# A transformer block on one core: the feed-forward's block 12 of the last tokens in row tiles of 64, and their last product, addition and store in two halves of columns

## The chip, the core and the metric

The kernel runs on one core of one Trainium2 chip. The metric is the device time in microseconds of one launch, input and output in device memory. A core has TensorE (PE; its weight loads are listed as PEld), VectorE (DVE), ScalarE (ACT), GpSimd (POOL) and SyncE (SP, which here issues all transfers); each works through a queue of its own, in order, and waits for the others through semaphores. TensorE writes its results into PSUM, eight banks of 2 KB in each of the 128 partitions.

## The reference

A transformer block on 2048 tokens of width 448: attention with 16 heads of 28 that share one key and one value head, then a gated feed-forward of width 1792, each behind a layer norm and with a residual. Cut to what matters:

```
def _A_ref(x, wq, wk, wv, wo):
    q = (x @ wq).reshape(B, S, H, Dh).transpose(0, 2, 1, 3)
    k, v = x @ wk, x @ wv
    p = softmax(einsum("bhqd,bkd->bhqk", q, k) * Dh ** -0.5)
    o = einsum("bhqk,bkd->bhqd", p, v)
    return o.transpose(0, 2, 1, 3).reshape(B, S, H * Dh) @ wo

def _B_ref(x, w1, w3, w2):
    h = silu(x @ w1) * (x @ w3)
    return h @ w2

h = x + _A_ref(_layernorm(x), wq, wk, wv, wo)
h2 = h + _B_ref(_layernorm(h), w1, w3, w2)
```

All is float32. To keep that accuracy the kernel splits an operand into a high part (rounded to the type `F32R`) and the rest, and adds up three products: high x high, low x high, high x low (`PAIRS3`).

## The kernel before

**Tiles.** The tokens are in NT = 4 tiles of T = 512 (index t), each of NQ = 4 groups of 128 tokens (index n). The width D = 448 is three chunks of 128 and one of 64. The feed-forward's 1792 hidden columns are NF = 14 blocks of 128 (index k). The attention comes first; the feed-forward follows as one loop over t and k, and the change touches its last two blocks, k = 12 and 13 of the last tile (`tl` = 3), and what stands behind the loop.

**One block.** For (t, k) there is a first product (x by w1 and by w3, into two PSUM banks of 512 columns), then `hidden` (L1030), then a second product with w2 that adds into the four banks Y[t][0..3], one for each group of 128 tokens, 448 columns used of 512. `hidden` is a chain over two engines: silu on ACT (L1032), multiplication on DVE (L1034), a copy that rounds to the high part on ACT (L1039), the subtraction for the low part on DVE (L1040). Its result goes into a buffer of `pt_ring` (L820), a ring of four of which each block takes two: first one for silu's result, then one for the high and low parts. Block k + 2 gets the buffers of block k again. A write to such a buffer waits for every earlier reader, also for one that is issued later in the program's text but belongs to the buffer's previous use.

**Two forms of a block.** The full form: `ffn1` (L1043) makes 2 x 11 matmuls of 128 rows through `mm_D` (L159; matmul L166), `ffn2` (L1065; matmul L1070) makes three matmuls for each n. The form in row tiles of 64: `ffn1_half` and `ffn2_half` (L1054, L1073) cut the 128 rows into two halves of 64 and issue pairs of matmuls, one on each half of the array, through `two` (matmul L1024); the two matmuls of a pair run side by side and write to different banks. Each is called twice, first with `late` = 0 and then with 1, and in the second call the two halves of rows have changed banks. `ffn1_half` has 11 pairs in the early and 10 in the late call, `ffn2_half` 6 in each. Since two halves of the array must not write one bank at the same time, each such call but the late one of `ffn1_half` ends with `settle` (L1027): ACT reads one element of the bank that was written last, and the next matmul into that bank waits for this read.

**The order around the change.** The order of every engine's queue is the order of the program's text. In a half block (t, k) it is: `ffn1_half` early, `ffn2_half` early of the block before, `ffn1_half` late, `hidden` of this block, then `rest()`, which is `ffn2_half` late of the block before; then `split_w2` (L488), which prepares this block's w2. So the second product lags one block behind. With the last tile the loop before takes blocks 0 to 11 in half form. Blocks 12 and 13 (`end`) are full: `ffn1(12)`, `ffn1(13)`, and the second products of 11, 12 and 13 stand behind the loop, all full. After each group n of the last product, `y_out` (L1087) adds the residual on DVE (L1092) and issues the store of X[tl][:, n] on SP (L1095).

```
    def settle(ps):
        se.activation(pexp[:1, 8:9], ps[:1, :1], AF.Copy)

        y, eng = Y[t][n][:, :D], ve
        eng.tensor_tensor(X[t][:, n], y, X[t][:, n], op=ALU.add)
        sy.dma_start(ov[t][:, n], X[t][:, n])
```

Of the kernel before, what the change touches and what calls it, by code (L numbers as in the profile page):

```python
# [11 lines left out]
ALU = mybir.AluOpType  # L12
# [4 lines left out]
P = 128  # L17
S = 2048
D = 448
# [5 lines left out]
NQ = T // P  # L25
NG = H // 4
NC = S // P
NF = F // P
# [7 lines left out]
def block_kernel(  # L36
# [13 lines left out]
    ve, se, ge, pe, sy = nc.vector, nc.scalar, nc.gpsimd, nc.tensor, nc.sync  # L50
    xv = x[0].rearrange("(t p n) d -> t p n d", t=NT, p=P, n=NQ)
    ov = out[0].rearrange("(t p n) d -> t p n d", t=NT, p=P, n=NQ)
# [14 lines left out]
    X = [keep.tile([P, NQ, D], F32, name=f"X{t}") for t in range(NT)]  # L67
# [75 lines left out]
    def bank(name="pb"):  # L143
        k = min(free, key=lambda k: order[k])
        free.remove(k)
        if k < 7:
            ps = ps_w.tile([P, T], F32, name=name, tag=f"bank{k}")
        else:
            ps = ps_o.tile([P, T], F32, name="po")
        used[id(ps)] = ps, k  # L150
        ready.pop(id(ps), None)
        return ps

    def done(ps, at=None):
        k = used.pop(id(ps))[1]
        order[k] = ready.get(id(ps), clock.end) + 0.7 if at is None else at
        free.append(k)
# [137 lines left out]
    QS, MX, MR, PT, PO, WH, WS = {}, {}, {}, {}, {}, {}, {}  # L295
# [183 lines left out]
    def split_w(k):  # L479
        wh, wl = [qs_tile().rearrange("p a (c m e) -> p (a c) m e", c=2, m=2)  # L480
                  for b in range(2)]
        ve.tensor_copy(wh, W13[k])
        ge.tensor_tensor(wl, W13[k], f(wh), op=ALU.subtract)
        return wh, wl
# [3 lines left out]
    def split_w2(k, own=False):  # L488
        if own or not w2s_home and k == 0:
            w2s = qs_tile()[:, :, 16 : 16 + D]  # L490
        else:
            if not w2s_home:
                w2s_home.append(keep.tile([P, 2, 2, T], F32R, name="w2s", tag="ks1"))
            w2s = w2s_home[0][:, k % 2, :, 16 : 16 + D]
        ve.tensor_copy(w2s[:, 0], W2[k])
        ge.tensor_tensor(w2s[:, 1], W2[k], f(w2s[:, 0]), op=ALU.subtract)
        return w2s
# [380 lines left out]
    for s in range(AHEAD, LAST):  # L878
        i, c = divmod(s, NC)
        n, kt = divmod(c, NQ)  # L880
# [128 lines left out]
    HID, Y = {}, {}  # L1009
# [5 lines left out]
    PAIRS3 = ((0, 0), (1, 0), (0, 1))  # L1015
    FULL = 4
# [13 lines left out]
    def hidden(t, k, ps, then=None):  # L1030
        sg = f(pt_ring()[:, 0])
        se.activation(sg, ps[0], AF.Silu)  # L1032
        done(ps[0])
        ve.tensor_tensor(sg, ps[1], sg, op=ALU.mult)  # L1034
        done(ps[1])
        if then is not None:
            then()
        h = pt_ring()
        se.activation(h[:, 0], sg, AF.Copy)  # L1039
        ve.tensor_tensor(h[:, 1], sg, f(h[:, 0]), op=ALU.subtract)  # L1040
        HID[t, k] = h[:, 0], h[:, 1]

    def ffn1(t, k, W):  # L1043
        ps = [bank("pa"), bank("pa")]
        for m in range(2):
            mm_D(ps[m], ps[m], [w[:, :, 1 - m] for w in W], XT[t], slice(0, P), slice(0, T))
        hidden(t, k, ps)
# [6 lines left out]
    def ffn1_half(t, k, W, ps, late):  # L1054
        us = [products(t, W, late, 0), products(t, W, 1 - late, 1)]
        if not late:
            us[0].append((W[1][HALF[0], 3, 1], XD[t][HALF[0]]))
            us[1].append((W[1][HALF[1], 3, 0], XT[t][2][HALF[1], 3]))
        to = (ps[0], ps[1]) if not late else (ps[1], ps[0])
        two([[(to[h], *u, not late and x == 0, late and x == len(us[h]) - 1) for x, u in enumerate(us[h])]  # L1060
             for h in range(2)])
        if not late:
            settle(ps[1])

    def ffn2(t, k, n):  # L1065
        if n == 0 and k == 0:
            Y[t] = [bank() for _ in range(NQ)]
        hid, w2s = HID[t, k], WS[t, k]
        for m, (a, b) in enumerate(PAIRS3):
            pe.matmul(Y[t][n][:, :D], hid[a][:, n * P : (n + 1) * P], w2s[:, b],  # L1070
                      start=(k == 0 and m == 0), stop=(k == NF - 1 and m == 2), skip_group_check=True)

    def ffn2_half(t, k, late):  # L1073
        if k == 0 and not late:
            Y[t] = [bank() for _ in range(NQ)]
        hid, w2s = HID[t, k], WS[t, k]
        us = [[], []]
        for h in range(2):
            for n0 in (2, 0) if late else (0, 2):
                n, r = n0 + (h ^ late), HALF[h]  # L1080
                for m, (a, b) in enumerate(PAIRS3):
                    us[h].append((Y[t][n], hid[a][r, n * P : (n + 1) * P], w2s[r, b],
                                  not late and k == 0 and m == 0, late and k == NF - 1 and m == 2))
        two(us)
        settle(Y[t][0 if late else 3])

    def y_out(t, n):  # L1087
        y, eng = Y[t][n][:, :D], ve
        if t < NT - 1 and n > 1:
            y, eng = ln_pool.tile([P, 512], F32, name="xn", bufs=4)[:, :D], ge  # L1090
            se.activation(y, Y[t][n][:, :D], AF.Copy)
        eng.tensor_tensor(X[t][:, n], y, X[t][:, n], op=ALU.add)  # L1092
        done(Y[t][n])
        if t == NT - 1:
            sy.dma_start(ov[t][:, n], X[t][:, n])  # L1095
        elif n == NQ - 1:
            sy.dma_start(ov[t], X[t])

    tl = NT - 1
# [5 lines left out]
    def call(*at):  # L1105
        for fn, args in after.get(at, []):
            fn(*args)
# [24 lines left out]
    prev = None  # L1132
    for t in range(NT):
        for k in range(NF):
            end = t == tl and k >= NF - 2
            t2, k2 = divmod(NF * t + k + 2, NF)
            if t2 < NT:
                WH[t2, k2] = split_w(k2)
            W = WH.pop((t, k))
            if t == 0 and k < FULL or end:  # L1140
                ffn1(t, k, W)
                call(t, k)
                if prev is not None and not end:
                    for n in range(NQ):
                        ffn2(*prev, n)
            else:
                ps = [bank("pa"), bank("pa")]
                ffn1_half(t, k, W, ps, 0)
                ffn2_half(*prev, 0)
                ffn1_half(t, k, W, ps, 1)  # L1150

                def rest():
                    ffn2_half(*prev, 1)
                    if prev[1] == NF - 1:
                        for n in range(NQ):
                            y_out(prev[0], n)

                hidden(t, k, ps, rest if prev[1] == NF - 1 else None)
                call(t, k)
                if prev[1] != NF - 1:  # L1160
                    rest()
            t2, k2 = divmod(NF * t + k + 1, NF)
            if t2 < NT:
                WS[t2, k2] = split_w2(k2, end)
            call(t, k + 0.5)
            prev = (t, k)
    for n in range(NQ):
        ffn2(tl, NF - 3, n)
    for n in range(NQ):
        ffn2(tl, NF - 2, n)  # L1170
    for n in range(NQ):
        ffn2(tl, NF - 1, n)
        y_out(tl, n)


# [26 lines left out]
```

## Time and profile before

| | |
|---|---|
| median of three runs | 1160.41 us (1159.94 to 1161.62) |
| the profiled execution | 1160.38 us |
| its span, first to last instruction | 1158.6 us |
| granted TensorE clock, mean | 1.000 |
| stores of the last tile | 4 issues, 224 KB each |

The span lies within the profiled execution's own time; 1.8 us are outside it. In the profile's rows a line such as `PE L1024 MATMUL pb<-w2s,pt 64*128 64x448 f32 x7` names the engine, the line of the kernel, the operation, the tile written and the tiles read, rows by columns of the array used, the shape of the moving operand and the count; ahead of it stand the start in the span and the time from the first one's start to the last one's end, both in microseconds. In brackets behind it stands the idle time of the engine ahead of it and what ended that. A matmul's record covers its way through the array, so neighbours overlap; their pace is the distance of their starts. A number in brackets behind a windows column counts instructions. The PSUM tiles `pa`, `pb` and `po` are banks under the names that they were first given: Y[tl][0] is listed as `po` and Y[tl][1..3] as `pb` at the end, `pt` is a buffer of the ring, `pexp` the place that `settle` writes to.

### The profile page before, as it was taken

How to read it: one execution, taken by the hardware profiler on the slowest of the kernel's cores; microseconds unless marked ns; L12 is line 12 of the kernel's file. 1: busy time of each engine (PE TensorE's matmuls, PEld its weight loads, DVE VectorE, ACT ScalarE, POOL GpSimd, SP SyncE). 2: the span in 40 equal slices, each digit the busy share in tenths (PEclk: the TensorE clock that was granted, in tenths of full speed). 3: DMA queues.
4: the chain of work that ended last, by engine and by line, in shares of the span. 5: the costliest groups of instructions: out<-in, count | busy, mean ns of one | idle time of the engine just before them, and what ended most of it. 6: DMA issues, size and time to landing. Idle time of an engine off the chain costs nothing.

```text
span 1158.6 us, 25640 instructions
## 1 busy us (share of the span) xinstructions
PE 1149.0 (99%) x10154; PEld 772.7 (67%) x10154; DVE 805.8 (70%) x1498; ACT 764.3 (66%) x1587; POOL 330.2 (29%) x242
## 2 busy tenths in 40 slices
PE   8999999999999999999999999999999999999998
PEld 6664444446444445444445444589999999999997
DVE  8878999897999998999988983163543444344333
ACT  5649999997999997999997999512222222222221
POOL 5312001101101111110111011345565556556552
PEclk9999999999999999999999999999999999999999
DMA  4010100001000002000012100143211101000000
GB/s 168 10 38 1 34 13 18 19 15 47 19 12 10 19 24 54 19 20 3 19 24 55 50 19 14 56 103 96 73 39 20 41 1 49 17 33 33 1 1 33
DMA packets 66680, 38.15 MB, mean 33 GB/s; under 512 B 41728, under 2 KB 59392, under 8 KB 66560
## 3 DMA queue, kind: packets, MB, share of 16 engines
q1 hardware_dynamic: 66560, 36.51, 11.5%
q8 instruction: 79, 1.29, 0.5%
q14 instruction: 41, 0.34, 0.1%
HBM read 24.04 MB, written 7.47 MB: 27 GB/s over the span
## 4 chain that ended last, share of the span: by engine, by line
PE 94%; ACT 2%; DVE 2%; issue 1%; DMA 1%; SPq 0%; POOL 0%; ACTq 0%; POOLq 0%
PE po L423 21%; PE pb L407 20%; PE pa L1024 18%; PE pa L323 10%; PE pb L1024 9%; PE pa L166 5%; PE pb L166 4%; PE po L1024 4%; PE pb L1070 1%; ACT OT L430 1%; ACT ab L344 1%; DVE mx L333 1%; PE pb L273 0%; ACT pt L414 0%; PE po L166 0%
## 5 line engine op out<-in xcount | busy, mean ns | idle before, releaser
L333 DVE TENSOR_REDUCE mx<-pa 128x1 f32<-128x512 f32 x689 | 440.1, 685 | 22.1 <-PE pb L407 13.0
L407 PE MATMUL pb<-qs,KS 32*128 32x512 f32 x3072 | 384.9, 425 | 0.0
L414 ACT ACTIVATE pt<-pb 128x512 f32<-128x512 f32 x684 | 365.9, 621 | 20.1 <-PE pb L407 17.3
L407 PEld LDWEIGHTS pb<-qs,KS 32*128 32x128 f32 x3072 | 234.0, 182 | 132.2 <-ACT pt L414 66.9
L323 PE MATMUL pa<-KS,qs 32*128 32x512 f32 x886 | 311.7, 459 | 1.3
L1024 PE MATMUL pa<-xl,qs 64*128 64x512 f32 x1044 | 195.4, 388 | 0.0
L323 PEld LDWEIGHTS pa<-KS,qs 32*128 32x128 f32 x886 | 138.6, 182 | 83.6 <-DVE mx L333 46.3
L423 PE MATMUL po<-pt,VA 128*32 128x512 f32 x1368 | 182.2, 605 | 0.4 <-ACT pt L414 0.4
L1024 PE MATMUL pa<-xh,qs 64*128 64x512 f32 x739 | 159.9, 388 | 0.0
L454 POOL TENSOR_TENSOR OT<-OT,rb 128x512 f32<-128x512 f32 x15 | 19.7, 1311 | 458.1 <-DMA rb<-sd 240.9
L1024 PE MATMUL pb<-w2s,pt 64*128 64x448 f32 x1050 | 145.2, 360 | 0.0
L1034 DVE TENSOR_TENSOR pt<-pa,pt 128x512 f32<-128x512 f32 x49 | 33.8, 691 | 159.0 <-ACT pt L1032 152.9
L1024 PEld LDWEIGHTS pa<-xl,qs 64*128 64x128 f32 x1044 | 141.9, 184 | 3.1
L1024 PEld LDWEIGHTS pb<-w2s,pt 64*128 64x128 f32 x1050 | 125.2, 184 | 2.0 <-DVE pt L1040 0.2
L351 DVE CUSTOM_DVE_ANT_0 ab<-pa,ab 128x512 f32<-128x512 f32 x138 | 93.6, 686 | 39.5 <-PE pa L323 28.4
L1024 PEld LDWEIGHTS pa<-xh,qs 64*128 64x128 f32 x739 | 108.4, 184 | 3.2
L414 ACT ACTIVATE xl<-pb 128x512 f32<-128x512 f32 x170 | 99.6, 610 | 8.9 <-PE pb L407 6.8
L414 ACT ACTIVATE xh<-pb 128x512 f32<-128x512 f32 x170 | 104.5, 633 | 0.0
L1032 ACT ACTIVATE pt<-pa 128x512 f32<-128x512 f32 x49 | 29.3, 597 | 94.7 <-PE pa L1024 90.9
L423 PE MATMUL po<-xl,VA 128*32 128x512 f32 x340 | 89.4, 605 | 0.0
L423 PE MATMUL po<-xh,VA 128*32 128x512 f32 x340 | 89.4, 605 | 0.0
L344 ACT ACTIVATE ab<-pa 128x512 f32<-128x512 f32 x138 | 82.2, 608 | 6.7 <-PE pa L323 4.9
(156 smaller groups left out, 1411.4 us busy)
## 6 DMA issues: line engine op xcount, KB each, us to landing
rb<-sd SPq DMA_DIRECT2D x64, 64.0 KB
xr<-xn SPq DMA_DIRECT2D x64, 56.0 KB
QR<-OT SPq DMA_DIRECT2D x60, 56.0 KB
QR<-in_B_w_dram SPq DMA_DIRECT2D x16, 192.0 KB
xh<-xr SPq DMA_DIRECT2D x4, 768.0 KB
X<-in_A_x_dram SPq DMA_DIRECT2D x3, 896.0 KB
out_dram<-X SPq DMA_DIRECT2D x3, 896.0 KB
w<-in_B_w_dram SPq DMA_DIRECT2D x8, 192.0 KB
```

Source lines behind the costliest of these rows:

```text
L166: pe.matmul(ps, lhs[b][:, cb, lsl], (rhs[2] if ca == 3 and len(rhs) == 3 else rhs[a])[:, ca, rsl], start=(k == 0), stop=(k == len(terms) - 1),
L323: pe.matmul(ps, QS[i][r, 0, n * P : (n + 1) * P], KS[0][r, kt * T : (kt + 1) * T] if keys is None else keys[r], start=True, stop=True)
L333: ve.tensor_reduce(self.to(), ps, axis=AX.X, op=ALU.max)
L344: se.activation(self.ab, ps, AF.Relu)
L351: ve.tensor_tensor_reduce(self.ab, ps, self.ab, 1.0, -3.0e38, ALU.add, ALU.max, self.to())
L407: pe.matmul(self.ps, KS[k % 2][r, c * P : (c + 1) * P], QS[i][r, k // 2], start=(k == 0), stop=(k == 2))
L414: se.activation(f(PT[i, c, p][:, jj]), self.ps, AF.Exp, bias=0.0, scale=SCALE)
L423: pe.matmul(PO[i][32 * j : 32 * j + 32], VA[:, c], f(PT[i, c, j // 2][:, j % 2]), start=(c == 0), stop=(c == NC - 1))
L454: eng.tensor_tensor(o, o, rb, op=ALU.mult)
L1024: pe.matmul(ps[:, : rhs.shape[-1]], lhs, rhs, start=bool(first), stop=bool(last), skip_group_check=True)
L1032: se.activation(sg, ps[0], AF.Silu)
L1034: ve.tensor_tensor(sg, ps[1], sg, op=ALU.mult)
```

## The change

Block 12 of the last tile takes the half form: only block 13 is still full. Block 12's iteration does not call `rest()`, so the late half of block 11's second product moves behind the loop, behind `ffn1(13)` and `hidden` of 13, and is followed by the full second products of 12 and 13. Of the last product's group n = 3, the three matmuls, the addition and the store are each done twice, for columns 0 to 223 and 224 to 447, in the order matmuls, addition, store, matmuls, addition, store; both halves lie in the one bank of Y[tl][3].

```
@@ -1137,7 +1137,7 @@
             if t2 < NT:
                 WH[t2, k2] = split_w(k2)
             W = WH.pop((t, k))
-            if t == 0 and k < FULL or end:
+            if t == 0 and k < FULL or (t, k) == (tl, NF - 1):
                 ffn1(t, k, W)
                 call(t, k)
                 if prev is not None and not end:
@@ -1157,20 +1157,27 @@
 
                 hidden(t, k, ps, rest if prev[1] == NF - 1 else None)
                 call(t, k)
-                if prev[1] != NF - 1:
+                if prev[1] != NF - 1 and (t, k) != (tl, NF - 2):
                     rest()
             t2, k2 = divmod(NF * t + k + 1, NF)
             if t2 < NT:
                 WS[t2, k2] = split_w2(k2, end)
             call(t, k + 0.5)
             prev = (t, k)
-    for n in range(NQ):
-        ffn2(tl, NF - 3, n)
+    ffn2_half(tl, NF - 3, 1)
     for n in range(NQ):
         ffn2(tl, NF - 2, n)
-    for n in range(NQ):
+    for n in range(NQ - 1):
         ffn2(tl, NF - 1, n)
         y_out(tl, n)
+    hid, w2s = HID[tl, NF - 1], WS[tl, NF - 1]
+    for h in range(2):
+        sl = slice(h * D // 2, (h + 1) * D // 2)
+        y = Y[tl][NQ - 1][:, sl]
+        for m, (a, b) in enumerate(PAIRS3):
+            pe.matmul(y, hid[a][:, (NQ - 1) * P :], w2s[:, b, sl], start=False, stop=(m == 2), skip_group_check=True)
+        ve.tensor_tensor(X[tl][:, NQ - 1, sl], y, X[tl][:, NQ - 1, sl], op=ALU.add)
+        sy.dma_start(ov[tl][:, NQ - 1, sl], X[tl][:, NQ - 1, sl])
```

More of the change, by code (lines that the diff above doesn't have):

```diff
@@ L1139, in block_kernel @@
             W = WH.pop((t, k))
-            if t == 0 and k < FULL or end:
+            if t == 0 and k < FULL or (t, k) == (tl, NF - 1):
                 ffn1(t, k, W)
@@ L1159, in block_kernel @@
                 call(t, k)
-                if prev[1] != NF - 1:
+                if prev[1] != NF - 1 and (t, k) != (tl, NF - 2):
                     rest()
@@ L1166, in block_kernel @@
             prev = (t, k)
-    for n in range(NQ):
-        ffn2(tl, NF - 3, n)
+    ffn2_half(tl, NF - 3, 1)
     for n in range(NQ):
         ffn2(tl, NF - 2, n)
-    for n in range(NQ):
+    for n in range(NQ - 1):
         ffn2(tl, NF - 1, n)
         y_out(tl, n)
+    hid, w2s = HID[tl, NF - 1], WS[tl, NF - 1]
+    for h in range(2):
+        sl = slice(h * D // 2, (h + 1) * D // 2)
+        y = Y[tl][NQ - 1][:, sl]
+        for m, (a, b) in enumerate(PAIRS3):
+            pe.matmul(y, hid[a][:, (NQ - 1) * P :], w2s[:, b, sl], start=False, stop=(m == 2), skip_group_check=True)
+        ve.tensor_tensor(X[tl][:, NQ - 1, sl], y, X[tl][:, NQ - 1, sl], op=ALU.add)
+        sy.dma_start(ov[tl][:, NQ - 1, sl], X[tl][:, NQ - 1, sl])
 _INS = ["A_x", "A_wq", "A_wk", "A_wv", "A_wo", "B_w1", "B_w3", "B_w2"]
```

## The prediction

> **What bounds the kernel now.** I read the page first: its span, the busy row and the chain that ended last.
>
> ```profile
> span 1158.6 us, 25640 instructions
> PE 1149.0 (99%) x10154; PEld 772.7 (67%) x10154; DVE 805.8 (70%) x1498; ACT 764.3 (66%) x1587; POOL 330.2 (29%) x242
> PE 94%; ACT 2%; DVE 2%; issue 1%; DMA 1%; SPq 0%; POOL 0%; ACTq 0%; POOLq 0%
> ```
>
> TensorE is busy 99% of the span and carries 94% of the chain: a matmul taken off its queue, or a gap put into it, shows one to one. The change touches only the end, so next comes the chain of the last 21 us (start, length, what).
>
> ```profile
> 1137.51 10.19 PE pa L166 x44
> 1147.70 0.61 PE po L1070 x3
> 1148.31 1.80 PE pb L1070 x9
> ...
> 1152.51 0.61 PE po L1070 x3
> ...
> 1153.15 2.43 DVE X L1092 x4
> ```
>
> Blocks 12 and 13 (44 matmuls of 512 columns), then the second products of blocks 11, 12 and 13, 12 matmuls of 448 columns each: block 11's take 0.61 + 1.80 us, so 0.200 us a matmul. After 1153.15 the four additions set the end. Behind them stand the stores; the windows view gives the share of the DMA engines (last two columns: share, GB/s).
>
> ```profile
> core 0: us, PE busy (x) PEld busy (x) DVE busy (x) ACT busy (x) POOL busy (x), PEclk, DMA share, GB/s
> 1154.50:1155.00 0.50, 0.41 (x3) 0.04 (x1) 0.50 (x2) 0.00 (x0) 0.00 (x0) 1.00 0.67 251
> 1155.00:1155.50 0.50, 0.00 (x0) 0.00 (x0) 0.50 (x1) 0.00 (x0) 0.00 (x0) 1.00 1.03 380
> ...
> 1157.00:1157.50 0.50, 0.00 (x0) 0.00 (x0) 0.00 (x0) 0.00 (x0) 0.00 (x0) 1.00 0.23 83
> 1157.50:1158.60 1.10, 0.00 (x0) 0.00 (x0) 0.00 (x0) 0.00 (x0) 0.00 (x0) 1.00 0.00 0
> ```
>
> The engines move data from 1155.00 - 0.67 x 0.5 = 1154.67 to 1157.00 + 0.23 x 0.5 = 1157.12, without a pause. Four stores of 224 KB in 2.45 us are 374 GB/s, 0.61 us each; 1.48 us more pass to the end of the span.
>
> **Part 1: block 12 in row tiles of 64.** A half block's period is the distance of two silu starts; the pace of full matmuls comes from rows of blocks 12 and 13.
>
> ```profile
> 1129.11 0.60 ACT L1032 ACTIVATE pt<-pa 128x512 f32<-128x512 f32 x1 [1.79 <-PE pa L1024]
> ...
> 1136.33 0.60 ACT L1032 ACTIVATE pt<-pa 128x512 f32<-128x512 f32 x1 [2.07 <-PE pa L1024]
> ...
> 1136.94 0.57 PE L1024 MATMUL po<-w2s,pt 64*128 64x448 f32 x2
> ...
> 1137.43 0.53 PEld L166 LDWEIGHTS pa<-xl,qs 128*128 128x128 f32 x3 [0.31 <-issue]
> ...
> 1138.23 0.85 PE L166 MATMUL pa<-xh,qs 128*128 128x512 f32 x3
> ...
> 1146.40 0.84 PE L166 MATMUL pa<-xl,qs 128*128 128x512 f32 x3
> ...
> 1147.09 0.62 PE L166 MATMUL pa<-xh,qs 128*128 128x512 f32 x2
> ```
>
> Of the 44 matmuls 3 start before 1138.23 and 5 from 1146.40 on: 8.17 us / 36 = 0.227 us. Removed: 22 x 0.227 + 12 x 0.200 = 7.39 us. Added: one period, 7.22 us, with both of its halves of the second product. **Gain 0.17 us**: the 64 rows left over of 448 = 3 x 128 + 64 take 21 slots of pairs where full tiles take 22. Its own waits (the two settles, HID of the block before) stand where every half block has them, within the period.
>
> **Mode switches.** Before there is one, half to full. The second of the two matmuls at 1136.94 starts at 1137.14, so the next slot would be 1137.34; counted back from 1138.23 (3 x 0.227) it is 1137.55: 0.21 us. The other direction occurs once, behind the last wo_rows:
>
> ```profile
> 773.30 2.39 PE L166 MATMUL pa<-WO,OS 128*128 128x448 f32 x11
> ...
> 775.62 0.18 PEld L1024 LDWEIGHTS po<-xl,qs 64*128 64x128 f32 x1 [0.31 <-issue]
> ...
> 775.96 0.39 PE L1024 MATMUL po<-xl,qs 64*128 64x512 f32 x1
> ```
>
> The eleventh ends at 775.69, so starts at 775.33 (a matmul of 448 columns is 0.57 - 0.20, say 0.36 us long); its successor's slot would be 775.53, and is 775.96 - 0.23 = 775.73: 0.20 us. After the change the order is: half block 12, full ffn1 of 13, late half of block 11's product, full products of 12 and 13. Three switches for one: **+0.20 us** here, and one more that falls into the wait that follows.
>
> **The new wait.** ffn2_half ends with settle(Y[0]), a 1x1 read by ACT; the next matmul, ffn2(12, 0), writes Y[0] and has to wait for it. In ACT's queue settle stands behind the cast of block 13 (L1039), which is emitted earlier, in hidden(13). That cast writes the pt buffer that holds block 11's hidden (a ring of 4, two per block), so it can't start until the last matmul of block 11's product has read it:
>
> ```profile
> 1148.75 1.36 PE L1070 MATMUL pb<-w2s,pt 128*128 128x448 f32 x6
> ...
> 1150.15 0.63 ACT L1039 ACTIVATE pt<-pt 128x512 fp32r<-128x512 f32 x1 [4.24 <-PE pb L1070]
> ```
>
> Before, this costs nothing: block 12's product runs on meanwhile. After, TensorE itself waits for cast and settle. Their prices:
>
> ```profile
> 1137.69 0.63 ACT L1039 ACTIVATE pt<-pt 128x512 fp32r<-128x512 f32 x1 [0.76 <-DVE pt L1034]
> ...
> 1138.22 0.14 ACT L1028 ACTIVATE pexp<-po 1x1 f32<-1x1 f32 x1
> ```
> ```profile
> 857.04 0.81 DVE L1040 TENSOR_TENSOR pt<-pt 128x512 fp32r<-128x512 f32 x1 [0.21 <-ACT pt L1039]
> ...
> 857.90 0.18 PEld L1024 LDWEIGHTS po<-w2s,pt 64*128 64x128 f32 x1 [0.20 <-DVE pt L1040]
> 857.90 0.47 PE L1024 MATMUL po<-w2s,pt 64*128 64x448 f32 x1
> ```
>
> From the start S of the last half matmul: its end +0.36, cast starts +0.04 (1150.11 to 1150.15), settle starts +0.53 (1137.69 to 1138.22) and takes 0.14, the weight load follows +0.05 (857.85 to 857.90), and a matmul whose load was not ahead loses 0.11 (0.47 against 0.36, the length of a matmul of 448 columns). The next slot is S + 1.23 in place of S + 0.20: **+1.03 us**, the switch within it. Bounds: +0.20 if nothing waits, and 1.03; the rows name each link, so I take 1.03. Behind the waiting matmul stand all 24 of blocks 12 and 13. The other input of that cast, the multiplication (L1034), starts 0.10 us after ffn1's end and takes 0.69; block 11's late half ends 1.4 us after it (switch and 6 slots of 0.200), so the cast waits for TensorE, not for DVE. DVE's subtraction behind the cast has 2.4 us of block 12's product as cover. The skipped rest() frees 1.20 us of TensorE between block 12 and 13; silu and multiplication of 12 then lie beside ffn1 of 13 (5.0 us), which needs neither.
>
> Sum on TensorE: -0.17 + 0.20 + 1.03 = **+1.06 us** at the start of the last products.
>
> **Part 2: the last product in two halves of columns.** The rows:
>
> ```profile
> 21.75 1.75 PE L273 MATMUL pb<-ident,xn 128*128 128x128 f32 x14 [0.18 <-DVE xn L213]
> ```
> ```profile
> L1034 DVE TENSOR_TENSOR pt<-pa,pt 128x512 f32<-128x512 f32 x6 | 4.1, 691 | 23.0 <-ACT pt L1032 16.9 <-PE pa L166 6.1
> ...
> L1092 DVE TENSOR_TENSOR X<-pb,X 128x448 f32<-128x448 f32 x3 | 1.8, 626 | 0.0
> ```
> ```profile
> 1153.75 1.83 DVE L1092 TENSOR_TENSOR X<-pb,X 128x448 f32<-128x448 f32 x3
> 1153.80 2.14 SPq L1095 DMA_DIRECT2D out_dram<-X  x4
> ```
>
> The trace has no matmul of 224 columns. Transposes, with a full weight load and 128 columns each, go at most 1.75 / 14 = 0.125 us apart, and 0.200 less 224 x 0.42 ns (0.227 - 0.200 over 64 columns) is 0.11: I take 0.11 each, at most 0.20. An addition of 224 columns: 65 ns per 64 columns, so 626 - 228 = 0.40 us. By the clock of before: the three additions in the row start 0.60 us apart, so the third of the four ends at 1154.98, and addition A, though its matmuls end near 1154.65, runs from 1154.96 to 1155.36.
>
> Does the second half's product wait for A? It is emitted behind A and writes other columns of the same PSUM tile, one bank (2 KB a partition). The trace shows no such pair; the nearest rows are matmuls into a bank whose reader is not done:
>
> ```profile
> PEld pb L407 <- ACT pt L414: 66.9, 87, 0.8
> ```
>
> So between 0 and the full price I take the wait. Then: load 1155.41, slot 1155.52, third matmul 1155.74 to 1156.01 (0.36 less 224 x 0.42 ns), addition B 1156.03 to 1156.43. The first store is issued at 1153.80 and moves data from 1154.67, 0.87 us later; B's moves from 1157.32, 0.31 us, to 1157.63, where before it ends at 1157.12: **+0.52 us**. Store A (data from 1156.48) is done by then. Without the wait B's addition ends at 1155.74, its data at 1157.09, since the engines are full up to there: 0.0. Outer bounds: slots of 0.20 us for both halves would add 0.3; half-length packets may go slower, by the 512-byte loads (140 GB/s at a share of 0.48, so 292) 0.39 us in place of 0.31:
>
> ```profile
> 776.00:778.00 2.00, 2.00 (x20) 1.68 (x18) 0.95 (x2) 0.00 (x0) 0.97 (x1) 1.00 0.48 140
> ```
>
> SP has one issue more; four span 2.14 us at the pace of the additions that they wait for, and A's and B's come 0.4 us or more apart, so I cost it at nothing; without that cover it is one issue, at most 2.14 - 3 x 0.60 = 0.34 us.
>
> The Trainium skill, page "PSUM — Partial Sum Buffer", section "PSUM bank collisions raise a hardware error", speaks against this split: two engines may not touch one bank in the same 32 partitions at once, even in disjoint columns, so software has to guard by bank. By that rule the halves can't overlap and the total is the forecast; without it, it would be the first rival's. No run here shows it yet.
>
> **Sum.** 1.06 + 0.52 = +1.58 us. The profiled execution took 1160.38 us (span 1158.6), the median of the three is 1160.41: so **1162.0 us**, 0.14% more. About 0.2% (2.3 us) is what a measurement of this kernel can tell from no change; this stays within it.
>
> **Rivals.**
> 1. The halves overlap: +1.06 + 0.0, **1161.4 us**. For it: the columns are disjoint. Against it: one tile, one bank.
> 2. settle doesn't hold TensorE (it, or the cast, runs earlier): -0.17 + 0.20 + 0.20 + 0.52 = +0.75, **1161.1 us**. Against it: the 4.24 us row above.
> 3. Neither wait: +0.23, **1160.6 us**; the change then just does nothing that counts, since the slot saved is spent on switches and the split meets full DMA engines.
> 4. Slower beyond 0.2%: the gaps of 0.8 us and 0.6 us let the granted clock fall for the last products (about 4.9 us of slots). At half clock +4.9: +6.5 in all, **1166.9 us**. It decides from 0.75 us more, a clock below 4.9 / 5.65 = 0.87. Against it: around an idle microsecond at the start (6 to 7) the clock column reads 1.00.
>
> ```profile
> 6.00:7.00 1.00, 0.00 (x0) 0.00 (x0) 0.93 (x4) 0.60 (x1) 0.83 (x3) 1.00 1.08 395
> 7.00:8.00 1.00, 0.79 (x7) 0.79 (x8) 0.93 (x5) 0.16 (x1) 0.56 (x2) 1.00 0.92 133
> ```
>
> **Numbers.** Forecast 0.62, rivals 0.15, 0.08, 0.05 and 0.04, anything else 0.06. The range runs from just below rival 3 to the forecast with both outer bounds of part 2 (+0.4) and half of the 1.7 us by which the three runs differ: 1160.3 to 1163.2. Slower by over 0.2% (above 1162.7): rival 4, an eighth of the forecast through that spread, half of the rest: 0.15. Faster: 0.02, no mechanism found that saves 2.3 us. Within 0.2%: 0.83.
>
> **What would show it.** Right: ACT's cast of block 13 released by an L1024 matmul, settle behind it, then TensorE idle some 0.8 us before the first L1070; its first L1070 1.06 us after the place that block 12's product had; a gap before the last three matmuls released by DVE; an end of data 0.5 us further behind the first L1092. Wrong: the first L1070 follows the last L1024 within 0.4 us; six short matmuls in a row; a block 12 period other than 7.22 less the 1.20 of the late half; a clock below 1.00.

## The result and the profile after

| | before | after |
|---|---|---|
| median of 22 runs each | 1160.28 us | 1161.92 us |
| lowest to highest | 1159.71 to 1161.62 | 1161.43 to 1164.52 |
| ratio, with its 95% interval | | 1.0013 (1.0007 to 1.0019) |
| the profiled execution, its span | 1160.38, 1158.6 | 1162.54, 1160.8 |

The change costs 1.64 us by the medians, 0.14% (by the ratio 0.13%): less than the 0.2% that the prediction gives as what a measurement can tell from no change, yet the interval of the ratio leaves out 1. The forecast was 1162.0 us.

The two spans differ by 2.2 us, more than the change costs. The reason stands ahead of the change: block 11's multiplication (L1034) starts at 1136.96 us in the trace of before and here at

```profile
1137.52 0.69 DVE L1034 TENSOR_TENSOR pt<-pa,pt 128x512 f32<-128x512 f32 x1 [4.24 <-ACT pt L1032]
```

though up to there both programs issue the same. Such a shift differs from one execution to the next (1136.23 to 1137.98 us over the traces of this study), so the end is read in two distances: **a**, from this start to the first matmul of block 13's second product, and **d**, from there to the end of the stores' data. In the timeline of before:

```profile
1136.96 0.69 DVE L1034 TENSOR_TENSOR pt<-pa,pt 128x512 f32<-128x512 f32 x1 [4.24 <-ACT pt L1032]
...
1152.35 0.76 PE L1070 MATMUL po<-qs,pt 128*128 128x448 f32 x3
```

So before, a = 1152.35 - 1136.96 = 15.39 us and d = 1157.12 - 1152.35 = 4.77 us.

The timeline of after where the late half of block 11's product ends (start, length, what, in brackets the idle time and its end):

```profile
1150.36 0.36 PE L1024 MATMUL pb<-w2s,pt 64*128 64x448 f32 x1
1150.37 0.36 PE L1024 MATMUL po<-w2s,pt 64*128 64x448 f32 x1
...
1150.77 0.63 ACT L1039 ACTIVATE pt<-pt 128x512 fp32r<-128x512 f32 x1 [3.31 <-PE po L1024]
1151.30 0.14 ACT L1028 ACTIVATE pexp<-po 1x1 f32<-1x1 f32 x1
...
1151.49 0.50 PEld L1070 LDWEIGHTS po<-w2s,pt 128*128 128x128 f32 x3 [1.14 <-ACT pexp L1028]
1151.50 0.87 PE L1070 MATMUL po<-w2s,pt 128*128 128x448 f32 x3 [0.77 <-ACT pexp L1028]
...
1154.01 0.76 PE L1070 MATMUL po<-qs,pt 128*128 128x448 f32 x3
```

The reader sees the predicted chain link by link: the last half matmul, the cast released by it, settle 0.53 us behind the cast's start, and TensorE idle until settle is done. a = 1154.01 - 1137.52 = 16.49, 1.10 us more than before.

The chain of work that ended last shows the same by engine (start, length, what): ACT, which had no place in this stretch of it before, now bridges the gap (ACTq is ACT's sequencer).

```profile
1150.77 0.63 ACT pt L1039
1151.39 0.06 ACTq L1204
1151.45 0.04 issue
1151.50 0.87 PE po L1070 x3
```

The last product in the timeline, then the stores in the windows view:

```profile
1155.42 1.21 DVE L1092 TENSOR_TENSOR X<-pb,X 128x448 f32<-128x448 f32 x2
...
1155.81 0.49 PE L1178 MATMUL pb<-qs,pt 128*128 128x224 f32 x3
1156.55 0.38 DVE L1179 TENSOR_TENSOR X<-pb,X 128x224 f32<-128x224 f32 x1
1156.98 0.41 PEld L1178 LDWEIGHTS pb<-qs,pt 128*128 128x128 f32 x3 [0.87 <-DVE X L1179]
1156.98 0.59 PE L1178 MATMUL pb<-qs,pt 128*128 128x224 f32 x3 [0.69 <-DVE X L1179]
1157.04 1.33 SPq L1180 DMA_DIRECT2D out_dram<-X  x2
1157.61 0.39 DVE L1179 TENSOR_TENSOR X<-pb,X 128x224 f32<-128x224 f32 x1 [0.69 <-PE pb L1178]
```
```profile
1158.50:1159.00 0.50, 0.00 (x0) 0.00 (x0) 0.00 (x0) 0.00 (x0) 0.00 (x0) 1.00 0.35 118
1159.00:1159.50 0.50, 0.00 (x0) 0.00 (x0) 0.00 (x0) 0.00 (x0) 0.00 (x0) 1.00 0.45 152
```

The fourth short matmul stands still until addition A ends at 1156.93 (1156.55 + 0.38). The data end at 1159.00 + 0.45 x 0.5 = 1159.22: d = 5.21, 0.44 us more than before. Both together are 1.54 us of the 1.64 by the medians. The share of 0.35 is a hole ahead of the last store: before, the DMA engines had none.

### The profile page after: what moved, and what is told of

Its sections match the earlier page's. It is cut to its first block, busy times and chain, and to the rows that moved or that the text cites. A ratio compares the mean times of both kernels' runs of the same rounds, so it can differ in the third digit from the quotient of the medians.

```text
span 1160.8 us, 25718 instructions
## 1 busy us (share of the span) xinstructions
PE 1150.5 (99%) x10189; PEld 773.9 (67%) x10189; DVE 806.1 (69%) x1499; ACT 764.8 (66%) x1590; POOL 330.2 (28%) x242
## 4 chain that ended last, share of the span: by engine, by line
PE 95%; ACT 2%; DVE 2%; issue 1%; DMA 1%; SPq 0%; POOL 0%; ACTq 0%; POOLq 0%; DVEq 0%
PE po L423 21%; PE pb L407 20%; PE pa L1024 18%; PE pa L323 10%; PE pb L1024 9%; PE pa L166 5%; PE pb L166 4%; PE po L1024 4%; PE pb L1070 1%; ACT OT L430 1%; ACT ab L344 1%; DVE mx L333 1%; PE pb L273 0%; ACT pt L414 0%; PE po L166 0%
## 5 line engine op out<-in xcount | busy, mean ns | idle before, releaser
L1024 PE MATMUL pa<-xl,qs 64*128 64x512 f32 x1068 | 198.4, 388 | 0.0
L1034 DVE TENSOR_TENSOR pt<-pa,pt 128x512 f32<-128x512 f32 x49 | 33.9, 691 | 160.0 <-ACT pt L1032 157.7
```

The lines of the kernel that those rows point to most:

```text
L1024: pe.matmul(ps[:, : rhs.shape[-1]], lhs, rhs, start=bool(first), stop=bool(last), skip_group_check=True)
```

## The experiments

In the diffs "-" and "+" are against the kernel named. All distances are from the traces:

| run | L1034 of block 11 | first matmul of 13's product | end of data | a | d | time against before, 95% interval |
|---|---|---|---|---|---|---|
| before | 1136.96 | 1152.35 | 1157.12 | 15.39 | 4.77 | |
| after | 1137.52 | 1154.01 | 1159.22 | 16.49 | 5.21 | 1.0007 to 1.0019 |
| e1_half_only | 1137.98 | 1154.46 | 1159.30 | 16.48 | 4.84 | 0.9999 to 1.0017 |
| e2_split_only | 1137.91 | 1153.30 | 1158.53 | 15.39 | 5.23 | 1.0000 to 1.0018 |
| e3_banks_1230 | 1136.23 | 1151.87 | 1156.71 | 15.64 | 4.84 | 0.9997 to 1.0014 |
| e4_products_first | 1136.69 | 1152.08 | 1156.92 | 15.39 | 4.84 | 0.9993 to 1.0011 |
| e5_rest_in_place | 1137.36 | 1152.58 | 1157.36 | 15.22 | 4.78 | 0.9987 to 1.0005 |
| e6_settle_first | 1136.63 | 1152.66 | 1157.43 | 16.03 | 4.77 | 0.9995 to 1.0014 |
| e7_own_bank | 1136.30 | 1151.68 | 1156.54 | 15.38 | 4.86 | 0.9989 to 1.0008 |
| e8_first_and_last_cut | 1137.04 | 1152.66 | 1157.67 | 15.62 | 5.01 | 0.9994 to 1.0011 |

With 10 to 12 runs each the intervals of time are some 2 us wide and tell none of these kernels surely from before. The distances do: where a kernel leaves a stretch as it was, its a or d repeats within 0.1 us.

**The two parts alone.** e1 is the change with the last product as before:

```
-    for n in range(NQ - 1):
+    for n in range(NQ):
         ffn2(tl, NF - 1, n)
         y_out(tl, n)
-    hid, w2s = HID[tl, NF - 1], WS[tl, NF - 1]
...
```

> Part 1 alone: block 12 in half form as in the change, the last product unsplit as before. Two distances are read from each trace: a, from the start of block 11's multiplication (L1034) to the first matmul of block 13's second product, before 15.39 us, after 16.49; d, from there to the end of the stores' data, before 4.77, after 5.21. Theory (ACT's cast and settle hold TensorE behind block 11's late half, besides one switch more and one slot less): a 16.5, d 4.8, time +1.1 us against before. Rival (the tail makes most of the loss): a 15.4 to 15.6, time +0.2.

Measured: a 16.48, d 4.84, the medians 0.9 us apart (1161.27 against 1160.36). The whole of a's loss comes from part 1; the rival falls.

```profile
1151.95 0.88 PE L1070 MATMUL po<-w2s,pt 128*128 128x448 f32 x3 [0.77 <-ACT pexp L1028]
...
1155.33 0.62 DVE L1092 TENSOR_TENSOR X<-po,X 128x448 f32<-128x448 f32 x1 [2.76 <-PE po L1070]
```

d is 0.07 us longer than before, in e3 too: in e1, e3 and after the first addition starts 0.87 us behind the first matmul of 13's product (here 1155.33 - 1154.46), in before 0.80. Why is not shown. In the change this costs nothing at the end, since there the DMA engines wait ahead of the last store anyway.

e2 is the kernel before with the last product in halves as in the change.

> Part 2 alone: the last product in halves, blocks 12 and 13 full as before. Theory (the second half's matmuls wait for the first half's addition, which reads the same bank): a 15.4, d 5.2, a gap of about 0.7 us between the third and fourth short matmul, time +0.4 to +0.5 us. Rival (additions and packets of half length cost more, no wait): six short matmuls at 0.11 us, then a longer d all the same.

Measured: a 15.39, d 5.23, and the wait:

```profile
1155.10 0.49 PE L1179 MATMUL pb<-qs,pt 128*128 128x224 f32 x3
1155.84 0.38 DVE L1180 TENSOR_TENSOR X<-pb,X 128x224 f32<-128x224 f32 x1
1156.27 0.41 PEld L1179 LDWEIGHTS pb<-qs,pt 128*128 128x128 f32 x3 [0.87 <-DVE X L1180]
1156.28 0.59 PE L1179 MATMUL pb<-qs,pt 128*128 128x224 f32 x3 [0.69 <-DVE X L1180]
```

By d the loss is 0.46 us, about as in the change (0.44). One execution of e2 took 3657.59 us; no trace shows why. The median of the other ten (1161.44 against 1160.36) says 1.1, more than the trace accounts for; the interval covers both.

**What holds TensorE in part 1.** e3 is e1 with another order of the groups:

```
-    for n in range(NQ):
+    for n in (1, 2, 3, 0):
         ffn2(tl, NF - 2, n)
```

> Part 1 alone, but block 12's full product takes the groups in the order 1, 2, 3, 0, so that nine matmuls lie between block 11's late half and the first write to Y[0], the bank that settle reads. Theory: the wait for cast and settle is covered, only the switch is left, a 15.66 (0.83 less than with the order 0 to 3), time +0.25 us against before. Rival (the way back to full matmuls costs a microsecond, whatever bank comes next): a 16.5, time +1.1.

Measured: a 15.64, 0.84 us less than e1. Its timeline:

```profile
1149.36 1.71 PEld L1070 LDWEIGHTS pb<-w2s,pt 128*128 128x128 f32 x9 [0.30 <-issue]
1149.36 2.08 PE L1070 MATMUL pb<-w2s,pt 128*128 128x448 f32 x9
1149.47 0.63 ACT L1039 ACTIVATE pt<-pt 128x512 fp32r<-128x512 f32 x1 [3.31 <-PE po L1024]
1150.01 0.14 ACT L1028 ACTIVATE pexp<-po 1x1 f32<-1x1 f32 x1
```

Cast and settle are as late as ever behind the half matmuls, but nine matmuls into other banks run beside them: no gap but the switch. The rival, a dear way back to full matmuls, falls. e6 leaves TensorE's order and changes ACT's:

```
-    def ffn1(t, k, W):
+    def ffn1(t, k, W, then=None):
...
-        hidden(t, k, ps)
+        hidden(t, k, ps, then)
...
-                ffn1(t, k, W)
+                ffn1(t, k, W, (lambda: ffn2_half(tl, NF - 3, 1)) if t == tl else None)
...
-    ffn2_half(tl, NF - 3, 1)
```

> Part 1 alone with block 11's late half and its settle emitted inside hidden of block 13, behind the multiplication and ahead of the cast: TensorE's order is unchanged, ACT's has settle ahead of the cast. Theory (TensorE waits for cast and settle in ACT's queue): the cast's 0.53 us drop out, a 15.96, the gap on TensorE ends with settle 0.2 us behind the last half matmul. Rival (ACT's order doesn't matter, the switch or the buffer of the ring holds TensorE): a 16.5.

Measured: a 16.03, 0.45 us less than e1, of 0.53 expected.

```profile
1149.48 0.36 PE L1024 MATMUL po<-w2s,pt 64*128 64x448 f32 x1
...
1149.94 0.16 ACT L1028 ACTIVATE pexp<-po 1x1 f32<-1x1 f32 x1 [3.37 <-PE po L1024]
1150.00 0.61 ACT L1039 ACTIVATE pt<-pt 128x512 fp32r<-128x512 f32 x1
1150.15 0.50 PEld L1070 LDWEIGHTS po<-w2s,pt 128*128 128x128 f32 x3 [0.68 <-ACT pexp L1028]
```

settle now starts 0.10 us behind the last matmul's end (1149.84), where the cast, in the trace of after, started 0.04 behind it (1150.73 to 1150.77); that is most of the missing 0.08. The place in ACT's queue is thus a cause of its own: of the 0.84 us that e3 hides, 0.45 are the cast ahead of settle, and 0.39 (16.03 - 15.64) stay with settle alone, the way from the last half matmul over ACT back to TensorE.

**Block 12 in half form without the moved product.** e5 is e1 with rest() called in block 12 too:

```
-                if prev[1] != NF - 1 and (t, k) != (tl, NF - 2):
+                if prev[1] != NF - 1:
                     rest()
...
-    ffn2_half(tl, NF - 3, 1)
```

> Part 1 alone with rest() called in block 12 as in every other half block, so that block 11's late half lies ahead of block 13's first product: one switch, and settle(Y[0]) 5 us ahead of the next write to that bank. Theory: only the slot saved is left, a 15.22, d 4.8, time -0.17 us against before (too little for the interval). Rival (half form costs something of its own at this place, such as block 12's hidden coming late): a 15.4 or more.

Measured: a 15.22, d 4.78: the slot saved, 0.17 us, is all that is left. settle is over more than 4 us ahead of the next write to its bank, and TensorE does not wait:

```profile
1145.85 0.14 ACT L1028 ACTIVATE pexp<-po 1x1 f32<-1x1 f32 x1
...
1150.17 0.77 PE L1070 MATMUL po<-w2s,pt 128*128 128x448 f32 x3
```

It is the one kernel here whose end is shorter than that of before, by the trace; its time (1160.63 against 1160.36 by the medians, 0.9987 to 1.0005 by the ratio) can't show so little.

**What holds the end in part 2.** e4 is e2 with both halves' matmuls first:

```
     for h in range(2):
...
             pe.matmul(y, ...)
+    for h in range(2):
+        sl = slice(h * D // 2, (h + 1) * D // 2)
+        y = Y[tl][NQ - 1][:, sl]
         ve.tensor_tensor(X[tl][:, NQ - 1, sl], y, X[tl][:, NQ - 1, sl], op=ALU.add)
```

> Part 2 alone with both halves' matmuls ahead of both halves' additions and stores, so that no matmul stands behind an addition of its bank. Theory (bank wait): six short matmuls in a row at 0.11 us, d 4.7 to 4.9, time within 0.15 us of before. Rival (half-length additions and packets are the cost): d 5.1 or more.

Measured: d 4.84 and no gap.

```profile
1153.88 0.82 PE L1179 MATMUL pb<-qs,pt 128*128 128x224 f32 x6
1154.74 0.69 DVE L1183 TENSOR_TENSOR X<-pb,X 128x224 f32<-128x224 f32 x2
```

Additions and stores are as short as in e2, and the loss is 0.07 us in place of 0.46: it was the wait. e7 keeps the overlap and takes the shared bank away:

```
+    sl = slice(D // 2, D)
+    pb2 = bank()
+    ve.tensor_tensor(X[tl][:, NQ - 1, sl], Y[tl][NQ - 1][:, sl], X[tl][:, NQ - 1, sl], op=ALU.add)
...
+        y = pb2[:, sl] if h else Y[tl][NQ - 1][:, sl]
...
+            pe.matmul(y, ..., start=(h == 1 and m == 0), ...)
```

> Part 2 alone, with block 13's product for columns 224 to 447 of the last group in a bank of its own; what Y[tl][3] holds in these columns from blocks 0 to 12 is added to X by one more addition ahead of block 13's product. No matmul waits for an addition, and addition A lies beside the second half's product. Theory (DMA engines and DVE are full there): d 4.7 to 4.8, no gain over before. Rival (the split pays once the bank wait is gone): d 4.3 to 4.5.

Measured: d 4.86, a little above the 4.7 to 4.8 of the theory. The matmuls run through and the halves overlap, and nothing is gained. The windows of e7 say why:

```profile
1153.50:1154.00 0.50, 0.50 (x6) 0.50 (x5) 0.50 (x2) 0.00 (x0) 0.00 (x0) 1.00 0.04 14
1154.00:1154.50 0.50, 0.30 (x3) 0.12 (x2) 0.50 (x2) 0.00 (x0) 0.00 (x0) 1.00 0.96 351
...
1156.00:1156.50 0.50, 0.00 (x0) 0.00 (x0) 0.00 (x0) 0.00 (x0) 0.00 (x0) 1.00 0.98 333
1156.50:1157.00 0.50, 0.00 (x0) 0.00 (x0) 0.00 (x0) 0.00 (x0) 0.00 (x0) 1.00 0.07 22
```

Data begin 2.30 us behind the first matmul (1153.98), as before (1154.67 - 1152.35 = 2.32), and the engines are full to the end; an earlier last store only queues. The halves at the end move at 333 / 0.98 = 340 GB/s, where whole stores before, by the same division, moved at 380 / 1.03 = 369; for the 224 KB of the last group that is 0.05 us more, most of the 0.07 of e4 and a good half of the 0.09 here.

**A cut at both ends.** e8 is e5 with groups 0 and 3 both cut, each second half in a bank of its own.

> Block 12 in half form with rest() in its place, and the first as well as the last group of the last product in halves of columns, the second half of each in a bank of its own. Theory (the stores are one stream of 2.45 us that starts with the first addition, and the last addition ends together with it, so only both ends cut at once shorten it): a 15.22, first data about 0.4 us earlier behind the first matmul of block 13's product, d 4.4 to 4.5 (before 4.77), time -0.4 us against before, too little for the interval. Rival (the tail is set by something that neither cut touches): d 4.8.

A miss: a 15.62, d 5.01. These rows show where it went:

```profile
1152.13 0.38 DVE L1172 TENSOR_TENSOR X<-po,X 128x224 f32<-128x224 f32 x1
...
1152.66 0.56 PE L1183 MATMUL po<-qs,pt 128*128 128x224 f32 x3 [0.22 <-DVE X L1172]
...
1153.40 1.37 PE L1070 MATMUL pb<-qs,pt 128*128 128x448 f32 x6
...
1154.21 1.22 DVE L1092 TENSOR_TENSOR X<-pb,X 128x448 f32<-128x448 f32 x2 [0.22 <-PE pb L1070]
```
```profile
1155.83 0.45 SPq L1185 DMA_DIRECT2D out_dram<-X  x1
1156.38 0.41 SPq L1185 DMA_DIRECT2D out_dram<-X  x1
```
```profile
1155.40:1155.70 0.30, 0.03 (x1) 0.00 (x0) 0.30 (x3) 0.00 (x0) 0.00 (x0) 1.00 0.05 15
...
1157.20:1157.40 0.20, 0.00 (x0) 0.00 (x0) 0.00 (x0) 0.00 (x0) 0.00 (x0) 1.00 0.80 265
```

The early addition for group 0 reads the bank that the product writes next, and DVE comes to it only behind block 13's subtraction: a loses 0.4 us. d loses most on TensorE: group 0's six short matmuls take 0.74 us (1152.66 to 1153.40), where three whole ones took 0.60 before (1152.35 to 1152.95), so the addition of group 1 starts 1.55 us behind the first matmul (1154.21), before 1.40 (1153.75). The stream of stores does start earlier (2.0 us behind the first matmul), but runs dry until group 1's data come at about 1155.70, and is full from there to the end (a share of 1.00 from 1155.70 to 1157.20) but for a dip. The dip fits SP: the issue of one store takes 0.45 us there, and the last store is issued only at 1156.38, though its addition ended at 1156.03; by the share of 0.80 in 0.20 us I estimate 0.04 us for it. With the lower rate of the halves (0.05) these terms are 0.15 + 0.04 + 0.05 = 0.24, which is what d lost against before.

## Why the prediction was right, step by step

- **The total.** Forecast +1.58 us; 1.54 by a and d, 1.64 by the medians. The time alone would not carry the forecast: its interval, 0.8 to 2.2 us, also holds the +1.06 of rival 1, and that the medians fit within 0.1 us is in part luck. What shows the mechanism are the traces.
- **The slot saved, 0.17 us.** e5 has it alone: 15.39 - 15.22 = 0.17.
- **Three switches for one, 0.20 each.** e3 has the slot and two more switches: a is 0.25 longer, 0.23 by the terms (-0.17 + 0.20 + 0.20).
- **The wait for cast and settle.** Predicted S + 1.23 for the next slot; in after S is 1150.37, and the slot is 1151.50 + 0.11 = 1151.61: S + 1.24. The difference of e1 and e3, 0.84, is the wait beyond the switch; 0.83 was predicted. Rival 2 falls with the [1.14 <-ACT pexp L1028] row, rival 3 with it.
- **The sum on TensorE.** 1.06 predicted, 1.10 measured (a of after less a of before).
- **The bank wait.** It is there (rival 1 falls). As mechanism it was right, its size a little off: 0.44 in place of 0.52. Addition A starts closer behind the third addition than taken (1156.55, which is 0.08 before that one's end at 1156.63, in place of 0.02) and the short addition takes 0.38 and not 0.40. Counted from the first L1092, as the prediction's sign has it, the end of the data is only 0.37 us further behind (1159.22 - 1154.88 = 4.34 against 1157.12 - 1153.15 = 3.97), since that addition itself starts 0.07 us later. The Trainium skill, page "PSUM — Partial Sum Buffer", section "PSUM bank collisions raise a hardware error", asks for a guard by bank and quadrant of 32 partitions (by bank in the simple version) and not by address. The trace agrees as far as it can: the wait of 0.87 us on the weight load is between disjoint columns of one bank, and e7 with two banks has none. That is the program's guard at work; what the chip would do without it, no run here shows.
- **The split's own gain, nothing.** It was argued from the full DMA engines; e7 shows it without the wait.
- **SP's further issue at nothing.** Right for the change: store A is issued at 1157.04 and B, 1.33 us of both less 0.33 of its own later, at 1158.04, just behind addition B's end at 1158.00. In e8 that cover is gone and the last issue comes 0.35 us behind its addition's end, but earlier stores still fill the DMA engines, and by the windows it costs some 0.04 us.
- **Rival 4, a lower clock.** The windows of after show 1.00 up to the last store; the gaps of 0.77 and 0.69 us did not lower it. The argument against this rival was thinner than it looked: at the place at the start that it points to, where TensorE stood idle for 1.22 us before, e2's trace has 2.05 us of idle time and a fall of the clock behind it (last section).

## What to carry to other kernels

A wait is priced by the queue in which its release stands: a one-element read of 0.14 us cost 0.84, of which 0.45 because a copy that itself waited for TensorE stood ahead of it on ACT, and another order of the groups hid it all. Where the program guards PSUM by bank, as here, two halves of one bank are no double buffer: put the halves into two banks (e7), or finish all matmuls of the bank before its first reader (e4). Before splitting a last store, look whether the DMA engines have a hole in front of it; if they are full to the end, sending the last piece sooner gains nothing.

## What the runs showed of the hardware that was not expected

When TensorE has no more work its granted clock falls to 0.50, but at very different times. The windows of e2, whose last matmul ends at 1156.87, and of e5, whose last ends at 1155.15:

```profile
1157.50:1158.00 0.50, 0.00 (x0) 0.00 (x0) 0.00 (x0) 0.00 (x0) 0.00 (x0) 0.96 0.59 199
1158.00:1158.50 0.50, 0.00 (x0) 0.00 (x0) 0.00 (x0) 0.00 (x0) 0.00 (x0) 0.50 0.62 215
```
```profile
1157.00:1157.50 0.50, 0.00 (x0) 0.00 (x0) 0.00 (x0) 0.00 (x0) 0.00 (x0) 0.80 0.72 262
```

In e2 it falls at about 1157.96 (0.96 of 1 is the mean of a window with 0.04 us at half), 1.1 us behind the last matmul; in e5 at about 1157.30, 2.15 us behind; before, it is still 1.00 at the span's end, 3.7 us behind.

It also fell in front of more work. At 5 to 7 us of the program TensorE stands idle for 1.08 to 2.05 us, depending on the trace; in nine of the ten, with at most 1.66 us (e6), the clock stays at 1.00 there. In e2 it is 2.05 us:

```profile
7.27 0.78 PE L261 MATMUL pb<-ident,xn 128*128 128x128 f32 x4 [2.05 <-ACT xn L211]
```
```profile
7.50:8.00 0.50, 0.50 (x5) 0.50 (x4) 0.47 (x1) 0.00 (x0) 0.50 (x1) 0.67 0.54 80
8.00:8.50 0.50, 0.50 (x5) 0.50 (x4) 0.46 (x3) 0.19 (x1) 0.24 (x3) 0.50 0.12 16
```

The clock falls at about 7.67, 0.4 us after TensorE has gone on, and is back at about 11.08 (the window from 11.00 to 11.50 reads 0.92): 3.4 us at half. In e1's trace it is at half for 3.4 us too, from about 88.59 to 92.01 (0.59 in the window from 88.50, 0.99 in that from 92.00), though the windows show TensorE busy all around; why stays open. Executions with a lower mean clock are the long ones: e3's three with a mean clock of 0.995 to 0.997 took 1162.67 to 1164.44 us, against a median of 1160.31.

Two additions of 224 columns back to back take 0.69 us (e4), against 0.63 for one of 448: cutting an addition costs 0.06 us, less than the 0.15 us that the prediction's terms gave (0.40 + 0.40 less an overlap of 0.02).
